# Decode attention with grouped queries: semaphore waits carried by evictions and score matmuls instead of by instructions of their own

## The chip, the cores and the metric

The kernel runs on one core of one Trainium2 chip. The time is device microseconds from the start to the end of one execution; the figure compared is the median of several executions. The core has a matrix engine (TensorE, PE in the profile), three engines for elementwise work (VectorE or DVE, ScalarE or ACT, GpSimd or POOL), SyncE (SP), which here issues the loads, and 16 DMA engines that move data between HBM and on-chip memory. Each engine runs its own list of instructions in order; semaphores order them against each other.

## The reference

One decode step of attention: 32 query heads, each with one query of 128 elements, 8 key/value heads (four query heads share one) and 65536 keys and values per head, all bfloat16.

```python
B, Hq, Hkv, Sq, Sk, D = 1, 32, 8, 1, 65536, 128

def reference(q, k, v):
    rep = Hq // Hkv
    k = jnp.repeat(k, rep, axis=1)
    v = jnp.repeat(v, rep, axis=1)
    scores = jnp.einsum("bhqd,bhkd->bhqk", q, k) * D ** -0.5
    p = jax.nn.softmax(scores, axis=-1)
    return jnp.einsum("bhqk,bhkd->bhqd", p, v)
```

K and V are 134.2 MB each and every element is read once.

## The kernel before

**Units.** Each of the 8 key/value heads is cut into 4 chunks of 16384 keys, which makes 32 units (`NU`). Partition p of a chunk holds 128 consecutive keys, so a chunk of K or V is one load of 4096 KB into a tile of 128 partitions by 128 x 128 elements. `kbuf` and `vbuf` have two buffers each. SyncE asks for K of unit n+1, then V of unit n, and waits before a load until the buffer's former content has been used (`kfree`, `vfree`; lines 376 to 403). The first and the last K chunk come in two halves, the last V chunk in six pieces.

**Keys of a unit** (`pe_keys`). A tile is 128 keys; eight tiles make a group j, and 16 groups a unit. TensorE transposes the eight tiles of a group into one of four PSUM banks (`trb`, line 132). The bank is then copied to SBUF (`ktb`, room for eight groups) by VectorE (`tensor_copy`, line 219) or, where j mod 4 is 3, by ScalarE (`activation`, line 216); the function is `evict`. Three groups later (`LAG`) TensorE multiplies the eight transposed tiles, as weights, with the four queries of the head (`pe_scores`, line 141): eight matmuls that write the scores of the group into `qkb`. After the 16th group's transposes TensorE works off the three groups of scores that are still pending. So the next unit's transposes come behind all evictions of this one.

**Softmax and values.** VectorE takes the maximum over a unit's scores (line 248), GpSimd takes it across partitions (line 369), VectorE forms the running maximum and its difference to the last one, ScalarE does four exponentials with their sums (line 339), and TensorE multiplies the 128 tiles of V, as weights, with the probabilities (`value`, line 158; `pe_values`). On TensorE the values of a unit come after the keys of the next unit. VectorE adds them to `acc` (`add_values`). In VectorE's list a unit's 12 copies are cut into three parts, with the steps of the former unit's softmax between them (`dve_pass`); ScalarE's four stand around the exponentials (`act_pass`).

**The end.** `pe_last` takes the last unit's values piece by piece as they arrive, the last eight tiles with the operands the other way round, VectorE scales the last head's rows and SyncE writes them out (line 410).

**Loops and code.** TensorE loops 16 times over two units, with the start of the loop put at a chosen place in the code (`addr_align`). VectorE and ScalarE loop over four units, with some units before and after the loop; SyncE and GpSimd have no loop.

**Waits.** A wait in this kernel is `take` (lines 32 to 35): wait until a semaphore has reached n, then take n off it. The two become one instruction, which the profile lists under line 35, as a wait of the engine's sequencer (PEq, DVEq, ACTq). Four semaphores go with a group: `trd` and `tra` count groups that have been transposed, for VectorE and for ScalarE, and `evd` and `eva` count groups that VectorE and ScalarE have copied, for TensorE. In `evict` a `take` of one stands ahead of the copy, in `pe_scores` ahead of the eight matmuls. The signal that a K buffer is free (`kfree`) is given by ScalarE at group 15, between its `take` and its copy (line 215).

Of the kernel before, what the change touches and what calls it, by code (L numbers as in the profile page):

```python
# [6 lines left out]
AF = mybir.ActivationFunctionType  # L7
# [6 lines left out]
G = T // TB  # L14
NTB = 4
# [11 lines left out]

def on_act(j):
    return j % 4 == 3


def take(e, sem, n=1):

    e.wait_ge(sem, n)
    e.sem_inc(sem, -n)  # L35


def bass_standalone__gqa_softmax__decode_kernel(nc, q, k, v, out):
# [15 lines left out]
    def sem(name):  # L54
        return S(nc.semaphore(name))
# [32 lines left out]
    trb = [S(nc.psum_tensor(f"trb{i}", [P, TB * P], DT.bfloat16)) for i in range(NTB)]  # L88
# [8 lines left out]
    kfree = [sem(f"kfree{i}") for i in range(2)]  # L97
    vfree = [sem(f"vfree{i}") for i in range(2)]
    trd, tra, evd, eva = sem("trd"), sem("tra"), sem("evd"), sem("eva")
# [24 lines left out]
    def pe_transposes(pe, b, j):  # L124
        kv = kbuf[b][:, :].rearrange("p (t d) -> p t d", d=D)
        for i in range(TB):
            t = j * TB + i
            if t == 0:
                take(pe, krdy[b], 16)
            if t == HALF:  # L130
                take(pe, khalf[b], 16)
            ins = pe.transpose(trb[j % NTB][:, i * P:(i + 1) * P], kv[:, t, :], ident[:, :])  # L132
        ins.then_inc(tra if on_act(j) else trd, 1)

    def pe_scores(pe, b, j):
        take(pe, eva if on_act(j) else evd)
        if j == 0:
            take(pe, qrdy)
        for i in range(TB):
            t, off = j * TB + i, (j % NKG * TB + i) * P  # L140
            ins = pe.matmul(qkb[b][:, t * R:(t + 1) * R], lhsT=ktb[:, off:off + P],  # L141
                            rhs=qcur[:, :], start=True, stop=True)
        if j == G - 1:
            ins.then_inc(qkd, 1)

    def pe_keys(pe, b):
        pend = []
        for j in range(G):
            pe_transposes(pe, b, j)
            pend.append(j)  # L150
            if len(pend) > LAG:
                pe_scores(pe, b, pend.pop(0))
        while pend:
            pe_scores(pe, b, pend.pop(0))
# [54 lines left out]

    def evict(e, n, j):  # L210
        dst = ktb[:, j % NKG * TB * P:(j % NKG + 1) * TB * P]
        if on_act(j):
            take(e, tra)
            if j == G - 1:
                e.sem_inc(kfree[n % 2], 1)
            e.activation(dst, trb[j % NTB][:, :], AF.Copy).then_inc(eva, 1)  # L216
        else:
            take(e, trd)
            e.tensor_copy(dst, trb[j % NTB][:, :]).then_inc(evd, 1)  # L219

    def own(e, ins, s):
        ins.then_inc(s, 1)
# [18 lines left out]
    def dve_pass(e, u):  # L241
# [11 lines left out]
        if has_k(u):  # L253
            for j in part[0]:
                evict(e, u + 1, j)
# [10 lines left out]
        if has_k(u):  # L266
            for j in part[1]:
                evict(e, u + 1, j)
# [12 lines left out]
        if has_k(u):  # L281
            for j in part[2]:
                evict(e, u + 1, j)
# [163 lines left out]
```

## Time and profile before

| | |
|---|---|
| time, median of 3 runs | 633.25 us (633.08 to 633.67) |
| time of the profiled execution | 632.97 us |
| its span, first to last instruction | 631.2 us |
| mean granted TensorE clock | 0.772 of full |
| bytes read from HBM | 268.44 MB |
| TensorE, transposes (line 132), busy | 357.1 us, 4096 matmuls |
| TensorE, scores (line 141), busy | 173.3 us, 4096 matmuls |
| TensorE, values (line 158), busy | 112.1 us, 4088 matmuls |
| VectorE copies, mean of one | 691 ns, 384 of them |
| ScalarE copies, mean of one | 1023 ns, 128 of them |
| K chunk, issue to landing, median | 26.8 us |
| V chunk, issue to landing, median | 31.4 us |

How to read the lines that follow. The page cuts the span into 40 slices; a digit is the busy share of a slice in tenths, and GB/s is what the DMA engines moved in it. The list of DMA queues gives packets, MB and the share of 16 engines' time. A row of the waits says which line waited for what: total us, times, longest. A row of the timeline gives start and duration in us, engine, line, operation, tile written and tiles read, shapes, count, and in brackets the idle time before it and what ended it. PEld is TensorE's weight load, SPq an issue of a DMA by SyncE. A row of the groups gives busy us and mean ns, then idle us before the group. A row of the windows gives the stretch, its length, the busy time of PE, PEld, DVE, ACT and POOL with the number of instructions, the granted TensorE clock, the DMA engines' busy share, and GB/s. TensorE's work is pipelined, so its busy time runs above the time that the work takes up.

### The profile page before, as it was taken

The numbers are of one execution on the slowest core, as the hardware profiler recorded it, in microseconds if no ns is written. First come the engines' busy times: TensorE is split into PE (matmuls) and PEld (weight loads), VectorE is DVE, ScalarE is ACT, GpSimd is POOL, SyncE is SP. The second block draws the span as 40 slices with busy tenths as digits, with TensorE's granted clock in tenths as the row PEclk, the third lists the DMA queues.
The fourth block names the chain that finished last, engine by engine and source line by source line (L and its number), as shares of the span: only waits on it lengthen the run. The fifth ranks groups of instructions, "written<-read, shape, count | busy, mean of one in ns | idle before, by whom it ended". The sixth has DMA issues, their size and how long they took to land. (4 is left out here: it accounts for less than half of the span.)

```text
span 631.2 us, 27735 instructions
## 1 busy us (share of the span) xinstructions
PE 520.4 (82%) x12294; PEld 512.3 (81%) x12294; DVE 312.4 (49%) x689; ACT 182.4 (29%) x410; POOL 15.9 (3%) x49
## 2 busy tenths in 40 slices
PE   4579998879887798878798787988779887879897
PEld 4479997879887788877798787988779877779896
DVE  4445554446544456434565344654445544455552
ACT  2133322123322233221332213332223322133231
POOL 0000000000000000000000000000000000000000
PEclk9788776778776788767887677877678876788776
DMA  8999999999999999999999999999999999999996
GB/s 366 429 432 431 430 430 432 432 432 432 432 432 432 432 432 432 432 432 432 432 432 432 432 432 432 432 432 432 432 432 430 432 432 432 432 432 432 424 437 255
DMA packets 10335, 268.62 MB, mean 426 GB/s; under 512 B 1234, under 2 KB 1490, under 8 KB 1746
## 3 DMA queue, kind: packets, MB, share of 16 engines
q1 hardware_dynamic: 10232, 268.44, 99.1%
q8 instruction: 7, 0.11, 0.1%
q14 instruction: 6, 0.05, 0.0%
q10 hardware_dynamic: 90, 0.02, 0.0%
HBM read 268.44 MB, written 0.01 MB: 425 GB/s over the span
## 5 line engine op out<-in xcount | busy, mean ns | idle before, releaser
L132 PE MATMUL trb<-ident,kbuf 128*128 128x128 bf16 x4096 | 357.1, 246 | 76.1 <-PEq L35 73.3
L132 PEld LDWEIGHTS trb<-ident,kbuf 128*128 128x128 bf16 x4096 | 289.8, 112 | 78.0 <-issue 77.8
L219 DVE COPY ktb<-trb 128x1024 bf16<-128x1024 bf16 x384 | 255.2, 691 | 164.2 <-DVEq L35 163.5
L216 ACT ACTIVATE ktb<-trb 128x1024 bf16<-128x1024 bf16 x128 | 131.0, 1023 | 436.0 <-ACTq L35 436.0
L141 PE MATMUL qkb<-qcur,ktb 128*128 128x4 bf16 x4096 | 173.3, 165 | 22.5 <-PEq L35 20.5
L141 PEld LDWEIGHTS qkb<-qcur,ktb 128*128 128x128 bf16 x4096 | 156.3, 98 | 26.2 <-issue 26.0
L158 PE MATMUL pvb<-pts,vbuf 128*128 128x4 bf16 x4088 | 112.1, 165 | 4.9 <-issue 1.7
L158 PEld LDWEIGHTS pvb<-pts,vbuf 128*128 128x128 bf16 x4088 | 110.0, 101 | 6.8 <-issue 4.3
L339 ACT ACTIVATE pts<-qkb,negm 128x128 bf16<-128x128 f32 x128 | 50.8, 551 | 0.0
L248 DVE TENSOR_REDUCE cmax<-qkb 128x4 f32<-128x512 f32 x32 | 22.1, 692 | 35.2 <-DVEq L35 34.2
L339 ACT ACTIVATION_READ_ACCUMULATOR pts<-qkb,negm 128x1 f32 x128 | 36.1, 282 | 0.0
L237 DVE TENSOR_TENSOR acc<-acc,pvb 128x4 f32<-128x4 f32 x23 | 3.7, 159 | 59.8 <-DVEq L35 59.8
L369 POOL PARTITION_ALL_REDUCE cmaxa<-cmax x32 | 11.9, 370 | 506.3 <-POOLq L35 506.3
L235 DVE COPY acc<-pvb 128x4 f32<-128x4 f32 x8 | 1.3, 162 | 23.8 <-DVEq L35 23.8
L226 DVE COPY qcur<-qT 128x4 bf16<-128x4 bf16 x8 | 1.4, 170 | 10.0 <-DVEq L35 9.9
L278 DVE TENSOR_TENSOR lp<-lp,rsum 128x4 f32<-128x4 f32 x24 | 3.9, 163 | 3.5
L277 DVE TENSOR_TENSOR lp<-lp,alpha 128x4 f32<-128x4 f32 x24 | 3.9, 163 | 3.5
L264 DVE TENSOR_TENSOR dm<-m 128x4 f32<-128x4 f32 x24 | 3.9, 163 | 3.5
L335 ACT ACTIVATE alpha<-dm 128x4 f32<-128x4 f32 x24 | 4.7, 197 | 2.7 <-ACTq L35 2.7
L372 POOL PARTITION_ALL_REDUCE la<-lp x7 | 3.0, 429 | 97.0 <-POOLq L35 97.0
L198 PE MATMUL trb<-ident,qsb 32*128 32x32 bf16 x1 | 0.2, 204 | 5.1 <-DMA qsb<-in_q_dram 5.1
L198 PEld LDWEIGHTS trb<-ident,qsb 32*128 32x128 bf16 x1 | 0.1, 100 | 5.1 <-DMA qsb<-in_q_dram 5.1
(43 smaller groups left out, 32.7 us busy)
## 6 DMA issues: line engine op xcount, KB each, us to landing
vbuf<-in_v_dram SPq DMA_DIRECT2D x31, 4096.0 KB, 31.4
kbuf<-in_k_dram SPq DMA_DIRECT2D x30, 4096.0 KB, 26.8
kbuf<-in_k_dram SPq DMA_DIRECT2D x4, 2048.0 KB, 17.1
vbuf<-in_v_dram SPq DMA_DIRECT2D x1, 2048.0 KB, 17.7
vbuf<-in_v_dram SPq DMA_DIRECT2D x1, 1024.0 KB, 19.8
vbuf<-in_v_dram SPq DMA_DIRECT2D x1, 512.0 KB, 20.3
vbuf<-in_v_dram SPq DMA_DIRECT2D x1, 256.0 KB, 20.5
vbuf<-in_v_dram SPq DMA_DIRECT2D x2, 128.0 KB, 20.2
```

Source lines behind the costliest of these rows:

```text
L132: ins = pe.transpose(trb[j % NTB][:, i * P:(i + 1) * P], kv[:, t, :], ident[:, :])
L141: ins = pe.matmul(qkb[b][:, t * R:(t + 1) * R], lhsT=ktb[:, off:off + P], rhs=qcur[:, :], start=True, stop=True)
L158: return pe.matmul(pvb[b][:, 0:R], lhsT=vv[:, t, :], rhs=pts[b][:, t * R:(t + 1) * R], start=t == first, stop=t == last)
L216: e.activation(dst, trb[j % NTB][:, :], AF.Copy).then_inc(eva, 1)
L219: e.tensor_copy(dst, trb[j % NTB][:, :]).then_inc(evd, 1)
L248: e.tensor_reduce(cmax[:, :], qkb[u % 2][:, :].rearrange("p (t g) -> p g t", g=R), AX.X, ALU.max).then_inc(cm, 1)
L264: e.tensor_tensor(dm[:, :], mo[:, :], mn[:, :], ALU.subtract)
L277: own(e, e.tensor_tensor(lp[:, :], lp[:, :], alpha[:, :], ALU.mult), xd)
L278: own(e, e.tensor_tensor(lp[:, :], lp[:, :], rsum[:, :], ALU.add), xd)
L335: e.activation(alpha[:, :], dm[:, :], AF.Exp, scale=scale)
L339: ins = e.activation(pv[:, g, :], sv[:, g, :], AF.Exp, bias=negm[:, g:g + 1], scale=scale, accum_out=rsum[:, g:g + 1])
L369: e.partition_all_reduce(cmaxa[:, :], cmax[:, :], P, bass.bass_isa.ReduceOp.max).then_inc(cma, 1)
```

## The change

A new function `turn(j)` gives the place of group j, counted from 1, among the groups of a unit that the same engine copies, and whether it is the last of them (group 14 for VectorE, with count 12; group 15 for ScalarE, with count 4). The four semaphores are no longer brought back to zero after each group: they count up through the unit. The copy of a group, and the first of its eight score matmuls, carry a wait "at least k" themselves (`wait_op`). Only at the last group of each engine a `take` stands ahead, as before, and takes the whole count off.

```diff
+def turn(j):
+
+    same = [i for i in range(G) if on_act(i) == on_act(j)]
+    return same.index(j) + 1, j == same[-1]
...
     def pe_scores(pe, b, j):
-        take(pe, eva if on_act(j) else evd)
+        done, (k, last) = eva if on_act(j) else evd, turn(j)
         if j == 0:
             take(pe, qrdy)
+        if last:
+            take(pe, done, k)
         for i in range(TB):
             t, off = j * TB + i, (j % NKG * TB + i) * P
             ins = pe.matmul(qkb[b][:, t * R:(t + 1) * R], lhsT=ktb[:, off:off + P],
                             rhs=qcur[:, :], start=True, stop=True)
+            if i == 0 and not last:
+                ins.wait_op(done, k, "sem-ge")
         if j == G - 1:
             ins.then_inc(qkd, 1)
...
     def evict(e, n, j):
         dst = ktb[:, j % NKG * TB * P:(j % NKG + 1) * TB * P]
+        k, last = turn(j)
+        if last:
+            take(e, tra if on_act(j) else trd, k)
+        if j == G - 1:
+            e.sem_inc(kfree[n % 2], 1)
         if on_act(j):
-            take(e, tra)
-            if j == G - 1:
-                e.sem_inc(kfree[n % 2], 1)
-            e.activation(dst, trb[j % NTB][:, :], AF.Copy).then_inc(eva, 1)
+            ins = e.activation(dst, trb[j % NTB][:, :], AF.Copy).then_inc(eva, 1)
         else:
-            take(e, trd)
-            e.tensor_copy(dst, trb[j % NTB][:, :]).then_inc(evd, 1)
+            ins = e.tensor_copy(dst, trb[j % NTB][:, :]).then_inc(evd, 1)
+        if not last:
+            ins.wait_op(tra if on_act(j) else trd, k, "sem-ge")
```

## The prediction

> **What bounds the kernel now.** I read the slices of the page first, because a share over the whole span hides stages with different limits.
>
> ```profile
> span 631.2 us, 27735 instructions
> PE 520.4 (82%) x12294; PEld 512.3 (81%) x12294; DVE 312.4 (49%) x689; ACT 182.4 (29%) x410; POOL 15.9 (3%) x49
> ...
> DMA  8999999999999999999999999999999999999996
> GB/s 366 429 432 431 430 430 432 432 432 432 432 432 432 432 432 432 432 432 432 432 432 432 432 432 432 432 432 432 432 432 430 432 432 432 432 432 432 424 437 255
> ...
> q1 hardware_dynamic: 10232, 268.44, 99.1%
> ```
>
> The GB/s row is flat at 432 from the third slice to the 37th, and the data queue's packets fill 99.1% of 16 engines' span. A kernel held up by an engine would show dips where loads were asked for late. There are 32 units (a unit is one K chunk and one V chunk), so one takes 268.44 / 32 = 8.389 MB, or 19.4 us at 432 GB/s. All bytes need 621.4 us of the 631.2; the other 9.8 lie in the first slice, in the last, and in some 0.5 us of small dips between.
>
> Then the waits, to see which side is early, and one unit of TensorE without a wait in it, from the timeline:
>
> ```profile
> PE trb L132 <- PEq L35: 73.3, 28, 3.3
> ...
> PE qkb L141 <- PEq L35: 20.5, 55, 0.7
> ```
> ```profile
> 587.86 3.57 PE L132 MATMUL trb<-ident,kbuf 128*128 128x128 bf16 x32 [2.88 <-PEq L35]
> ...
> 604.80 3.57 PE L132 MATMUL trb<-ident,kbuf 128*128 128x128 bf16 x32
> ```
>
> TensorE stands before the first transposes of a unit 28 times, 73.3 us together, 2.6 us each: it waits for K. From 587.86 to the next unit's first transposes at 604.80, with no wait at either the values or the second start, is 16.9 us. So TensorE needs 16.9 us a unit and is supplied every 19.4: 2.5 us of slack a unit, which agrees with the 2.6 us of waiting.
>
> The last question is whether loads are asked for early enough that a shift of the engines cannot starve the DMA engines. SyncE's issues in the timeline:
>
> ```profile
> 0.73 0.88 SPq L382 DMA_DIRECT2D kbuf<-in_k_dram  x2
> ...
> 1.65 0.42 SPq L392 DMA_DIRECT2D kbuf<-in_k_dram  x1
> 2.20 0.66 SPq L402 DMA_DIRECT2D vbuf<-in_v_dram  x1
> 21.04 0.33 SPq L392 DMA_DIRECT2D kbuf<-in_k_dram  x1
> 21.47 0.37 SPq L402 DMA_DIRECT2D vbuf<-in_v_dram  x1
> 42.55 0.33 SPq L392 DMA_DIRECT2D kbuf<-in_k_dram  x1
> ...
> 605.12 3.02 SPq L382 DMA_DIRECT2D vbuf<-in_v_dram  x6
> ```
>
> Before the issue at 42.55 five chunks of 4.194 MB had been asked for, 20.97 MB; at 432 GB/s at most 18.1 MB can have moved since the first issue at 0.73. So at least 2.9 MB, 6.7 us of work, lay queued. At 605.12, when the last V chunk is asked for, 63 chunks (264.2 MB) had been asked for and at most 261.1 moved: 3.1 MB, 7.2 us. An issue may slip 6 us before the DMA engines have nothing to do. The kernel is bound by the bytes of K and V.
>
> **What the change removes, adds and moves.** Per unit, 16 groups of eight tiles go through TensorE and the evictions (12 on VectorE, 4 on ScalarE). Every group but the last of each evicting engine loses its own wait instruction: 14 on TensorE (16 less groups 14 and 15), 11 on VectorE, 3 on ScalarE, 28 a unit, 896 in 32 units. In their place 28 waits a unit ride on the first score matmul and on the copy. The last groups keep a wait that also takes off the whole count. No transfer, no tile and no arithmetic changes; the signal that frees the K buffer still follows ScalarE's last wait of a unit.
>
> *The removed waits on TensorE.* At full clock the weight loads show the rhythm:
>
> ```profile
> 615.15 0.30 PEld L141 LDWEIGHTS qkb<-qcur,ktb 128*128 128x128 bf16 x8
> 615.39 0.46 PEld L132 LDWEIGHTS trb<-ident,kbuf 128*128 128x128 bf16 x8
> 615.80 0.30 PEld L141 LDWEIGHTS qkb<-qcur,ktb 128*128 128x128 bf16 x8
> 616.03 0.46 PEld L132 LDWEIGHTS trb<-ident,kbuf 128*128 128x128 bf16 x8
> ...
> 618.32 3.46 PE L158 MATMUL pvb<-pts,vbuf 128*128 128x4 bf16 x128
> ```
>
> One group of scores and one of transposes take 0.65 us (615.15 to 615.80). Scores start 0.24 us before the transposes behind them; eight value matmuls of the same shape, with no wait between them, take 8 x 3.46 / 128 = 0.22. So a removed wait gives TensorE at most 0.02 us, 14 x 0.02 = 0.3 us a unit, and that only lengthens the wait for K at line 132. On the path that sets the end: 0.
>
> *The removed waits on VectorE and ScalarE.*
>
> ```profile
> 606.82 0.69 DVE L219 COPY ktb<-trb 128x1024 bf16<-128x1024 bf16 x1 [0.16 <-DVEq L35]
> ...
> 615.22 1.89 DVE L219 COPY ktb<-trb 128x1024 bf16<-128x1024 bf16 x3 [0.26 <-DVEq L35]
> ```
> ```profile
> L219 DVE COPY ktb<-trb 128x1024 bf16<-128x1024 bf16 x384 | 255.2, 691 | 164.2 <-DVEq L35 163.5
> L216 ACT ACTIVATE ktb<-trb 128x1024 bf16<-128x1024 bf16 x128 | 131.0, 1023 | 436.0 <-ACTq L35 436.0
> ```
>
> Where tiles are ready, three copies of 0.69 us run in 1.89 us without a gap, so the wait between them shows no cost; where TensorE is at half clock the gap is 0.16 us, and it is TensorE's pace. Bounds: 0 to 0.16 us a copy, 1.8 us a unit. I take 0, by the row of three copies. Either way VectorE idles 164.2 us and ScalarE 436.0 us before these instructions, so it gains nothing at the end.
>
> [...]
>
> *The added waits.* The trace has no compute instruction that carries its wait, so this price, call it c for each group on TensorE, is bounded by other rows. Lower end: minus 0.02 us, the gain above. Upper end: a whole exposed wait, line 141's 20.5 us / 55 = 0.37 us. Behind a carried wait on TensorE are queued the group's other seven matmuls and the next transposes, and for those VectorE waits. Nearest is the gapless rhythm of 615 us, where the copy is done long before its score is reached: I take 0. The cover is 2.5 us a unit in the middle, so c would have to pass 2.5 / 14 = 0.18 us there. At the end the cover is smaller:
>
> ```profile
> 622.03 0.16 DVE L237 TENSOR_TENSOR acc<-acc,pvb 128x4 f32<-128x4 f32 x1 [1.55 <-DVEq L35]
> ...
> 622.84 1.87 PE L158 MATMUL pvb<-pts,vbuf 128*128 128x4 bf16 x64 [0.82 <-DMA vbuf<-in_v_dram]
> ...
> 626.58 1.03 PE L158 MATMUL pvb<-pts,vbuf 128*128 128x4 bf16 x24 [0.21 <-DMA vbuf<-in_v_dram]
> 627.24 0.29 PEld L158 LDWEIGHTS pvb<-pts,vbuf 128*128 128x128 bf16 x8 [0.16 <-DMA vbuf<-in_v_dram]
> ```
>
> TensorE is ready for the last values at about 622.0 and waits for V pieces until 627.24; the 112 matmuls before that need 112 x 3.46 / 128 = 3.0 us. So 2 us of lateness in the last unit is hidden (c up to 0.15 us); behind 627.24 no instruction is edited.
>
> *The sum.* 0 + 0 + 0 on a path set by the bytes: span 631.2 as now. The profiled execution took 632.97 us, 1.8 more than its span; the median of three runs is 633.25 (633.08 to 633.67). I predict **633.2 us**.
>
> **Rivals.**
>
> *Carried waits hold TensorE up (slower).* The place is the first score matmul of 14 groups a unit, where a carried wait could keep its weight load from being read early. It decides from c = 0.15 us, at the end of the last unit, and from 0.18 in every unit. Halfway from there to the upper end, c = 0.26, a unit takes 16.9 + 3.6 = 20.5 us. With the first transposes at 8.3 us (where TensorE starts now), the last unit's keys start at 8.3 + 31 x 20.5 - 3.5 (no values in the first unit) = 640.3 instead of 604.80. From there to the end is 26.4 us now, plus 3.6, less the 2 hidden: 668.3, and with the 1.8 around it **670 us**. At c = 0.37 it would be about 720. For it: the price is not in this trace. Against: 2 us of cover on every side.
>
> ```profile
> 8.26 3.57 PE L132 MATMUL trb<-ident,kbuf 128*128 128x128 bf16 x32 [2.94 <-PEq L35]
> ```
>
> *TensorE's clock no longer recovers (slower).* One-microsecond windows of a unit:
>
> ```profile
> 603.00:604.00 1.00, 1.00 (x44) 1.00 (x41) 0.00 (x0) 0.00 (x0) 0.24 (x1) 0.50 0.92 393
> ...
> 609.00:610.00 1.00, 1.00 (x21) 1.00 (x19) 0.41 (x1) 1.00 (x5) 0.00 (x0) 0.64 0.84 360
> 610.00:611.00 1.00, 1.00 (x31) 1.00 (x29) 0.94 (x3) 1.00 (x8) 0.00 (x0) 1.00 1.07 459
> ```
> ```profile
> 608.17 0.40 PE L141 MATMUL qkb<-qcur,ktb 128*128 128x4 bf16 x8
> ...
> 609.23 0.40 PE L141 MATMUL qkb<-qcur,ktb 128*128 128x4 bf16 x8
> ```
>
> The granted clock (third number from the right) falls to 0.50 while values run, though TensorE is busy, and is 1.00 again five microseconds into the keys. At half clock a group takes 1.06 us (608.17 to 609.23). If the clock stayed there, a unit would be 3.4 + 12 x 1.06 + 1.8 + 3.5 = 21.4 us (start to first scores, twelve groups, drain, values), and the time by the same sum 8.3 + 31 x 21.4 - 3.5 + 26.4 + 21.4 - 16.9 + 1.8 = **701 us**. For it: the wait for K grows by up to 0.3 us. Against: the clock is already down when a unit starts, so a longer wait costs it nothing more.
>
> [...]
>
> *Loads get asked for earlier (faster).* All that an earlier issue can fill are the 0.5 us of dips: **632.5 us**, which still counts as no change. More than that needs the start or the tail shortened, and neither is edited.
>
> *It does not do what it says.* If each carried wait were turned back into an instruction of its own, the time would be 633.2 as well. The instruction count tells: 896 fewer.
>
> **How the numbers follow.** What a measurement of this kernel can tell from no change is about 0.2%, 1.3 us. Forecast, with the earlier loads and the unchanged program in it: 0.74. Carried waits: 0.15, a third of it at the small end where only the last unit is late (634.6 to 638). Clock: 0.04. A gain of over 1.3 us by something that no row shows: 0.07. So faster 0.07, same 0.74, slower 0.19. The range runs from 632.3 (the dips filled, and the spread of the runs) to 638 (the small end of the first rival), which leaves out the large ends of both slower cases and the unexplained gain, 0.2 together. The likeliest case's own range is 632.3 to 634.
>
> **What would show it.** Right: GB/s flat at 432, span near 631, about 26,840 instructions, waits before line 132's transposes at 2.5 to 3 us a unit, granted clock unchanged in shape. First rival: those waits go to nothing, idle at the score matmuls grows past 2 us a unit, GB/s drops below 420. Clock rival: 0.50 through whole key stages. Wrong altogether: a time over 1.3 us away with the GB/s row still flat at 432, for then the end is set by something that I have not read.

## The result and the profile after

The changed kernel takes 632.13 us (median of 21 runs, 631.93 to 632.27) against 633.14 us before (21 runs beside them, 632.88 to 633.67): ratio 0.9984, 95% interval 0.9978 to 0.999. It is 1.0 us faster, a difference that no two runs of the two kernels contradict, and that the predicted range (632.3 to 638.0) does not hold. The page of the changed kernel, the rows that answer to those of before:

```profile
span 630.3 us, 26839 instructions
...
GB/s 365 430 434 428 433 430 433 433 433 433 433 433 433 430 433 433 433 430 433 433 433 430 433 433 430 430 429 433 430 429 433 430 433 433 433 433 430 426 434 279
...
q1 hardware_dynamic: 10232, 268.44, 99.2%
q8 instruction: 7, 0.11, 0.1%
q14 instruction: 5, 0.04, 0.0%
```

There are 896 instructions fewer, as counted. The rate is as flat as before, but the last slice reads 279 GB/s instead of 255. And one row that the prediction passed over has moved: the queue q14, which the page lists as one of instructions (packets, MB, share of 16 engines' time). Before it was

```profile
q14 instruction: 6, 0.05, 0.0%
```

TensorE's waits in the changed kernel (line, what it waited for, total us, times, longest):

```profile
PE trb L138 <- PEq L41: 76.1, 30, 3.2
...
PE qkb L149 <- PEq L41: 20.8, 32, 0.7
```

It waits for K at the first transposes as it did (2.5 us a time). At the score matmuls this row counts only the waits that are still instructions. All idle time ahead of them, whatever ended it, is in the rows of the groups, before and after: 22.5 and 22.7 us.

```profile
L141 PE MATMUL qkb<-qcur,ktb 128*128 128x4 bf16 x4096 | 173.3, 165 | 22.5 <-PEq L35 20.5
```
```profile
L149 PE MATMUL qkb<-qcur,ktb 128*128 128x4 bf16 x4096 | 172.8, 165 | 22.7 <-PEq L41 20.8
```

VectorE's copies now show the transposes themselves as what they wait for, since the wait is the copy's own:

```profile
DVE ktb L230 <- PE trb L138: 154.9, 179, 3.9
```

So neither engine got slower or came nearer to the bound. The end of the chain that ended last tells where the microsecond is. Before, then after (start, us, what):

```profile
606.74 20.45 DMA vbuf<-in_v_dram
627.19 0.05 issue
...
629.22 0.34 DVE olast L326
```
```profile
606.46 19.85 DMA vbuf<-in_v_dram
626.31 0.05 issue
...
628.34 0.34 DVE olast L339
```

The load in this chain is the fourth of the six pieces of the last V chunk, the last for which TensorE has to stand; it is what is called the last landing below, and the last V piece in the expectations. It comes at 626.31 instead of 627.19 us, 0.88 earlier, and every step behind it follows by as much. Yet the last V chunk was asked for at the same moment (605.12 before, 605.13 after), and summed over all DMA engines the bytes moved are the same to within 0.1 us of work at every microsecond from 50 to 600. What changed is not how much the 16 engines move, but how far the last of them is behind the others. A piece lands in 16 shares, and the profile counts it as landed at the last of them. Of the sixth piece, before, the 15th share landed at 626.84 us and the 16th, with it the piece, at 627.85; after, at 626.83 and 626.96.

The packets of the trace show it. They are listed without their engine. But data packets follow each other closely (where only one packet ends near the start of another, it ends 3 to 4 ns after that start in nearly all cases, in both traces), which is taken here as the sign of one engine, so a delay can be followed. Before the change, in the middle of the last loads (start and end in us, bytes, queue):

```
604.918 605.537 16384 q1     data, 0.619 us (others of 16 KB: 0.61 to 0.62)
605.533 605.857  8192 q14    instructions
605.845 607.118 16384 q1     data, 1.273 us
607.114 607.725 16384 q1     data, 0.611 us
```

A read of 8 KB of instructions comes between two data packets of one engine. It took 0.31 us itself, and the packet behind it 0.66 us longer than the others: 0.97 us in all. The completion writes that end the loads, one for each engine and piece, show how far behind that engine is:

```
last six completion writes, us
before   626.24  626.27  626.37  626.73  627.07  627.41
after    626.15  626.18  626.18  626.20  626.40  626.53
```

Before, the last three, 0.34 us apart, are those of the last three pieces of V, each a microsecond behind the other 15 of its piece: they belong to one engine. After, there is no 8 KB read between 473 us and the last landing.

### The profile page after: what moved, and what is told of

It reads as the page before. It is cut to its first block, busy times and chain, and to the rows that moved or that the text cites. A ratio compares the mean times of both kernels' runs of the same rounds, so it can differ in the third digit from the quotient of the medians.

```text
span 630.3 us, 26839 instructions
## 1 busy us (share of the span) xinstructions
PE 521.5 (83%) x12294; PEld 513.8 (82%) x12294; DVE 312.9 (50%) x689; ACT 182.6 (29%) x410; POOL 15.9 (3%) x49
## 5 line engine op out<-in xcount | busy, mean ns | idle before, releaser
L149 PE MATMUL qkb<-qcur,ktb 128*128 128x4 bf16 x4096 | 172.8, 165 | 22.7 <-PEq L41 20.8
```

## The experiments

**Theory A**: VectorE's code got shorter by 88 instructions (11 in each of the eight unit bodies that its code holds), and therefore it no longer needs the 8 KB block that was read at 605.5 us (taken as 128 instructions; the runs below show one read more for 128 more). The read cost the DMA engine that carries it a microsecond, 0.97 us in the trace, and this engine lands last. In form A1 it does not matter when the read comes, since no engine has a pause in which to catch up; in form A2 only a late one counts. **Theory B**: TensorE's shorter code is through its first pass earlier, so loads are asked for earlier (the third K chunk at 19.82 us instead of 21.04, the fourth at 39.98 instead of 42.55), and that lead is kept. **Theory C**: each removed instruction gives its share.

### Each part of the change alone

Score matmuls only:

```diff
 kernel before, with in pe_scores
-        take(pe, eva if on_act(j) else evd)
+        done, (k, last) = eva if on_act(j) else evd, turn(j)
...
+        if last:
+            take(pe, done, k)
...
+            if i == 0 and not last:
+                ins.wait_op(done, k, "sem-ge")
```

> Only the score matmuls on TensorE carry their waits; both kinds of copies wait as before. Theory A (VectorE's shorter code no longer needs the 8 KB of instructions that were read at 605.5 us, in the middle of the last loads, on one of the 16 DMA engines): VectorE's code is as long as before, so the 8 KB read stays near 605 us, the last V piece lands near 627.2 us in the profile, and the time is that of before, 633.1 us (632.9 to 633.4). Theory B (TensorE's shorter code gets through its first pass earlier, loads are asked for 1.2 to 2.6 us earlier in the first 45 us, and this is kept to the end): the whole gain is here, 632.1 us. Theory C (each removed instruction gives its share): 14 of 28, so 632.6 us.

Measured: 633.08 us (11 runs), ratio 1.0001 (0.9992 to 1.001). SyncE's issues in its timeline:

```profile
20.05 0.33 SPq L402 DMA_DIRECT2D kbuf<-in_k_dram  x1
20.48 0.37 SPq L412 DMA_DIRECT2D vbuf<-in_v_dram  x1
38.80 0.33 SPq L402 DMA_DIRECT2D kbuf<-in_k_dram  x1
```

The loads are asked for earlier here too, the fourth K chunk even at 38.80 us, and nothing comes of it: B falls. An 8 KB read at 605.52 us is still there, and the last landing is at 627.18.

VectorE's copies only:

```diff
 kernel before, with in evict
-            take(e, trd)
-            e.tensor_copy(dst, trb[j % NTB][:, :]).then_inc(evd, 1)
+            k, last = turn(j)
+            if last:
+                take(e, trd, k)
+            ins = e.tensor_copy(dst, trb[j % NTB][:, :]).then_inc(evd, 1)
+            if not last:
+                ins.wait_op(trd, k, "sem-ge")
```

> Only VectorE's copies carry their waits (11 fewer instructions a unit, 88 fewer in VectorE's code). Theory A: no 8 KB instruction read after 480 us, one fewer in all, last V piece lands 0.9 us earlier, near 626.3 us, and the whole gain of 1.0 us is here: 632.1 us (631.9 to 632.4). Theory B: nothing, 633.1 us, since TensorE's code is that of before. Theory C: 11 of 28, 632.7 us.

Measured: 632.16 us (11 runs), ratio 0.9986 (0.9977 to 0.9995). The page's row of instruction reads and the chain's last load:

```profile
q14 instruction: 5, 0.04, 0.0%
```
```profile
606.68 19.73 DMA vbuf<-in_v_dram
```

The whole gain is in this part, and the last landing is at 626.41 us. ScalarE's copies only (the same edit at `tra` and `activation`):

> Only ScalarE's copies carry their waits (3 fewer instructions a unit). Theory A, with the read at 605.5 us taken to be VectorE's: 633.1 us and the 8 KB read near 605 us still there; if the read were ScalarE's, the whole gain would be here, 632.1 us. Theory B: 633.1 us. Theory C: 3 of 28, 633.0 us.

Measured: 633.10 us, ratio 0.9999 (0.999 to 1.0008), with an 8 KB read at 605.01 us. C falls with these three: against the 633.09 us of the kernel before in the same series the parts give 0, 0.9 and 0, not shares.

### The code's length without the waits

The changed kernel, with instructions on VectorE that do nothing for the result:

```diff
 changed kernel, in vector_engine
+        for _ in range(78):
+            e.sem_inc(padded, 1)
         passes(e, lambda u: dve_pass(e, u), 1, HU, NU - 4)
```

> The changed kernel with 78 instructions added on VectorE, once, ahead of its first unit (each adds 1 to a semaphore that nothing reads). They shift VectorE's code so that its third boundary of 128 instructions comes where it came before the change, in the pass that starts near 605 us. Theory A: an 8 KB instruction read near 605 us is back, the last V piece lands near 627.2 us and the gain is gone: 633.1 us (632.8 to 633.4; 632.4 if the DMA engine that it falls on is one that is not late). Theories B and C: the loops are those of the changed kernel and 78 instructions run once, so 632.1 to 632.2 us.

Measured: 633.05 us, ratio 1.0 (0.9991 to 1.0009). All waits are carried as in the changed kernel, and the gain is gone. Its instruction reads and its last load:

```profile
q14 instruction: 6, 0.05, 0.0%
```
```profile
606.23 21.05 DMA vbuf<-in_v_dram
```

The sixth read is back, at 605.01 us, and the last landing is at 627.28. The added instructions also put off the third K chunk's load, to 25.41 us; the runs further down do without that. To show that the loss comes from the read and not from the 78 instructions, fewer of them:

> The changed kernel with 36 of the same added instructions on VectorE instead of 78. The third boundary of its code then falls into the last steps, after the last load has landed. Theory A (a read of VectorE's code during the loads costs one DMA engine about 1 us, and this engine lands last): no 8 KB read between 480 and 626 us, 632.1 us (631.9 to 632.4). If the added instructions themselves had cost the microsecond of the run with 78: 632.6 us.

Measured: 633.05 us (632.35 to 633.63). The expectation missed: the boundary was reached sooner than I had placed it, and the 8 KB were read at 626.18 us, beside the very last pieces. Of its 11 runs two are at 632.4 and the others at 632.9 to 633.6. One more run has six fewer:

> The changed kernel with 30 added instructions on VectorE instead of 36. With 36 the third boundary of its code was reached at the wait ahead of the last steps, and the 8 KB were still read beside the last pieces of V, at 626.2 us. Six fewer put the boundary behind VectorE's last instruction. Theory A: no 8 KB read between 480 us and the last landing, last V piece near 626.3 us, 632.1 us (631.9 to 632.5). If added instructions as such cost the microsecond: 633.1 us.

Measured: 632.33 us (632.05 to 633.13), ratio 0.999 (0.9981 to 0.9999). In its profile the read comes at 626.71 us, behind the last data packet of all, which ends at 626.70 (the last landing is at 626.50); eight of 11 runs are at 632.05 to 632.4, three near 633.0, as if the read still fell among the last pieces now and then, which no profile of those three shows. The added instructions, with a read that came behind the data, cost 0.2 us (632.33 against 632.13).

### How many reads, and when

If 128 instructions are a block, 128 added ones leave every boundary where it lay and have one more block read early. The rows of q14 below show that one: 6 packets against the 5 of the changed kernel, 7 against the 6 of before.

> The changed kernel with 128 added instructions on VectorE ahead of its first unit: every boundary comes where it comes without them, and one more block of code is read, at about 8 to 15 us. Theory A1 (a read costs its DMA engine 1 us whenever it comes, since no engine has a pause before the end in which to catch up): three reads of VectorE's code during the loads as before the change, but none near 605 us, and 633.1 us (632.8 to 633.4). Theory A2 (only a read in the last 25 us counts, an earlier one is made up for by the loads still queued): 632.1 us.

Measured: 633.11 us (632.97 to 634.62), ratio 1.0005 (0.9996 to 1.0014), as A1 has it. But the run is not clean: VectorE needed so long for the added instructions that the third K chunk was asked for only at

```profile
29.09 0.33 SPq L408 DMA_DIRECT2D kbuf<-in_k_dram  x1
```

and packets of 32 KB that start between 31.6 and 33 us take up to 2.1 us instead of 1.21. The kernel before with the same 128:

> The kernel before with the same 128 instructions on VectorE: four reads of its code during the loads, one of them near 605 us. Theory A1: one more microsecond, 634.1 us (633.7 to 634.4), the last V piece near 628.2 us. Theory A2: 633.1 us.

Measured: 634.65 us (7 runs, 634.18 to 636.8), ratio 1.0033 (1.0021 to 1.0045), outside what either form expected. Its rate row shows why:

```profile
GB/s 364 436 428 387 431 433 436 431 431 431 431 433 431 433 431 431 433 431 433 431 433 431 435 431 431 431 429 431 433 431 431 433 431 433 433 435 431 420 431 263
```

The fourth slice, 387 GB/s, is a pause of most engines: near 51.7 us only 6 of the 16 have a data packet. The loads did run dry, and this counts as a run on something else. Both were repeated with the 128 split, 36 ahead of the first unit and 92 behind the first two passes, where VectorE has time for them:

> The changed kernel with 128 added instructions on VectorE again, but 36 ahead of its first unit and 92 behind the first two passes, so that the load of the third K chunk is asked for as early as in the changed kernel (near 20 us instead of 29) and the DMA engines have no pause at 31 us. Theory A1 (a read costs its engine 1 us whenever it comes): three reads of VectorE's code, none near 605 us, 633.1 us (632.8 to 633.4). Theory A2 (only late reads count): 632.1 us.

> The kernel before with the same 36 and 92 instructions: four reads of VectorE's code during the loads, and no pause of the DMA engines that would muddle the count. Theory A1: 634.1 us (633.7 to 634.4), the last V piece 1 us behind that of before. Theory A2: 633.1 us.

Measured: 633.18 us (633.07 to 633.29), ratio 1.0001 (0.9992 to 1.001), and 634.16 us (633.99 to 634.79), ratio 1.0018 (1.0009 to 1.0027). The first has the third K chunk asked for at 20.64 us, a flat rate, and 253 GB/s in the last slice, as before the change (255):

```profile
GB/s 365 430 435 432 430 432 430 432 432 432 432 432 432 430 432 432 432 432 432 432 432 432 432 432 432 432 432 432 432 432 432 432 432 432 432 432 432 423 435 253
...
q14 instruction: 6, 0.05, 0.0%
```

Its extra read is at 13.57 us, 614 us before the end of the loads, and there is none between 475 us and that end. Yet one engine is late as before the change: the last completion writes are at 626.35, 626.86, 627.20 and 627.55 us, and the last landing is at 627.32. So the read at 13.57 us cost as much as the one at 605 us before the change (633.18 and 633.14 us). That is A1; A2 falls. The second:

```profile
q14 instruction: 7, 0.06, 0.0%
```
```profile
606.91 21.52 DMA vbuf<-in_v_dram
```

Four reads of VectorE's code, last landing at 628.43 us, 1.2 later than in the kernel before with three. Two, three and four reads of VectorE's code during the loads give 632.13, 633.14 and 634.16 us.

Last, the same read on another engine's account: 128 added instructions on ScalarE.

> The changed kernel with 128 added instructions on ScalarE ahead of its first unit: one more 8 KB read, of ScalarE's code. Theory A, with each instruction queue's reads on a DMA engine of their own: ScalarE's engine finishes about a microsecond before the last one in the changed kernel, and the read costs it 0.7 us, so the last landing stays and the time is 632.1 us (631.9 to 632.5). If any 8 KB read on any engine cost the loads a microsecond: 633.1 us.

Measured: 632.16 us (632.09 to 632.34), ratio 0.9985 (0.9976 to 0.9994). Its q14 row is that of before:

```profile
q14 instruction: 6, 0.05, 0.0%
```

There are as many 8 KB reads as before the change, and the gain stays. So here, with six reads each and 632.16 against 633.14 us, not the number of reads decided but, by the landings, the engine that carried them. The 16 landings of the sixth piece show it: in the changed kernel nine engines are through by 625.93 us and seven come at 626.50 to 626.96; with ScalarE's extra read, eight by 625.89 and eight at 626.50 to 627.09. One engine has moved into the late group, without becoming the last.

In one table, by reads of VectorE's code while loads run:

| kernel | reads | us |
|---|---|---|
| changed; VectorE part alone; changed, ScalarE longer | 2 | 632.13; 632.16; 632.16 |
| changed, 30 added | 2, and one about the last landing | 632.33 |
| changed, 36 added | 2, and one among the last pieces | 633.05 |
| before; TensorE part alone; ScalarE part alone | 3 | 633.14; 633.08; 633.10 |
| changed, 78 added; 128 added (two ways) | 3 | 633.05; 633.11 and 633.18 |
| before, 128 added (split) | 4 | 634.16 |
| before, 128 added at once, loads ran dry | 4 | 634.65 |

The page of each kernel lists instruction reads on two queues: q8, 7 of 16 KB, taken here to be TensorE's, and q14, all of 8 KB, among them VectorE's and ScalarE's. They did not pass the loads by: VectorE's cost the engine that carried them 0.93 to 0.97 us each. Nor does TensorE seem to be spared. In its first 50 us before the change it stands four times with no wait that the profile shows:

```profile
18.16 0.33 PE L141 MATMUL qkb<-qcur,ktb 128*128 128x4 bf16 x7 [0.91 <-issue]
31.64 0.44 PE L132 MATMUL trb<-ident,kbuf 128*128 128x128 bf16 x5 [2.81 <-issue]
39.16 0.19 PE L141 MATMUL qkb<-qcur,ktb 128*128 128x4 bf16 x2 [1.05 <-issue]
46.32 3.09 PE L158 MATMUL pvb<-pts,vbuf 128*128 128x4 bf16 x111 [1.69 <-issue]
```

Each time it goes on 1.3 to 1.5 us after the end of a 16 KB read (at 16.83, 30.32, 37.71 and 45.01 us). In the changed kernel there are two such stops, 1.41 and 0.23 us. That would be why its third and fourth K chunks are asked for earlier. It is read off these times and was not tested, and it costs nothing here: with the fourth K chunk asked for at 38.80 instead of 42.55 us the time was 633.08 against 633.14 us.

## Why the prediction was wrong

**What bounds the kernel** was right as to the resource: the bytes of K and V set the time, TensorE waits for K in every unit, and with the same number of reads of VectorE's code, loads asked for 1 to 4 us earlier or later change nothing (the third K chunk at 20.05, 21.04 and 25.41 us: 633.08, 633.14 and 633.05 us). But "the data queue's packets fill 99.1% of 16 engines' span" was read as if the 16 were one. A load counted as landed with the last of its 16 shares (the sixth piece at 627.85 us), and 99.1% says nothing of how unequal the engines are: in the kernel before, one was 1.0 us behind the next.

**The removed waits**: 0 on TensorE and on ScalarE, as predicted (633.08 and 633.10 us with these parts alone). **The added waits**: c was taken as 0 within minus 0.02 and 0.37 us; all idle time ahead of the score matmuls went from 22.5 to 22.7 us over 32 units, so the mean of c over the 448 edited groups is below 0.01 us. VectorE's carried waits as such are worth 0 as well: with them and the old position of the code the time is 633.05 us.

**The step that failed** is the sentence "No transfer, no tile and no arithmetic changes". Code was a transfer here too. The page had the row, q14 with 6 packets and 0.05 MB at 0.0%, and I gave it no term. The missing term is one read less, 0.97 us on the engine that lands last, and the sum would have been 633.25 - 0.97 = 632.3 us, or 632.2 from the 633.14 of 21 runs, against 632.13 measured. The 0.0% hid its size: it is a share of the time of all 16 engines, and the end followed the last one, which was 1.0 us late.

**The rivals.** Carried waits that hold TensorE up, and a clock that does not recover, did not occur: line 138 waits 2.5 us a unit, the weight loads of the score matmuls start 0.05 us ahead of them in both kernels (median of the groups), and the granted clock is 0.767 against 0.772. That a longer wait lowers the clock, for which the forecast gave 0.04, no run shows; both traces have it at 0.50 from 603 to 604 us, with TensorE busy, and at 1.00 from 610 to 611. Loads asked for earlier were worth nothing, not the 0.5 us of dips. "More than that needs the start or the tail shortened, and neither is edited" is wrong: the tail did get 0.9 us shorter, through the length of VectorE's code. The chance of 0.07 was for a gain of over 1.3 us "by something that no row shows"; this gain is smaller, and a row did show its cause. By the prediction's own measure a change of less than 0.2%, 1.3 us, counts as none, which was the likeliest case. That the gain stays within it is luck: the sum had no term for it. The 0.2% was also too coarse for this kernel: VectorE's part alone, 0.14% faster, was told from nothing by 11 runs.

## What to carry to other kernels

In a kernel that keeps all DMA engines busy from start to end (here 99.1% of the span), count the instruction reads of each engine (the page's instruction queues) as transfers: here each delayed one DMA engine by 0.7 to 1.5 us, and on the engine that was last nothing made up for it before the last landing. A change that only shortens or lengthens code can then move the time in whole steps, as here by 1.0 us for each read of VectorE's code (632.13, 633.14 and 634.16 us), whatever it does otherwise; test it by adding idle instructions to the new version until the old boundary is back. When a load-bound time moves and the rate row does not, look at the last landing and at which packets stand between the data of the engine that lands last.

## What the runs showed of the hardware

- An 8 KB instruction read cost its DMA engine 0.97 us in VectorE's case: 0.31 us for itself and 0.66 us on the data packet behind it. The three other 8 KB reads during the loads of the kernel before cost 0.65 to 0.72 us. 128 instructions more on VectorE or on ScalarE, one read more (q14 with 6 packets for 5, or 7 for 6).
- The six reads of 16 KB between 13 and 50 us, taken to be TensorE's, show as gaps of 0.96 to 1.05 us and 0.47 to 0.55 us on the next packet, some 1.5 us each, and on different engines. In the changed kernel the sixth piece's completion writes come at 626.07 to 626.53 us on seven engines and at 624.5 to 625.5 on the others. So the next thing in the way would be those reads: if the last engine is still the one with VectorE's, one read of VectorE's less would bring only 0.1 us (626.53 to 626.40), by an estimate from these ends. No kernel without the 16 KB reads was tried.
- VectorE's reads seem to have fallen on one and the same engine, as far as packets can be followed (three in the kernel before, 0.93 to 0.97 us each); why this one, and how queues are given to engines, stays open.
